# Attention with key chunks of 128: the last 64 keys of two head pairs on four quarters of the array, sums of four heads at once, order laid out by four heads

## The chip, the cores and the metric

The kernel runs on one core of one Trainium2 chip. The metric is the device time of one execution in microseconds. Each kernel was executed several times; all executions told of here are in the fast state (with one core there is nothing to tell a slow one by except its time, and all executions of each kernel lie within 0.5% of each other). The profile is one such execution. Its span runs from the first to the last instruction and is some 2 us shorter than the device time (1043.4 against 1045.3 us for the kernel before). Comparisons of stages below use spans, comparisons of kernels use device times.

## The reference, cut to what matters

Attention with normalised queries and keys, then a feed-forward block with the activation SoLU, all in fp32:

```python
# q, k, v: (8, 12, 448, 64)
q_n, k_n = rmsnorm(q, g_q), rmsnorm(k, g_k)
scores = scale * np.matmul(q_n, k_n.transpose(0, 1, 3, 2))      # 448 x 448 for each of 96 heads
attn = np.exp(scores - scores.max(-1)); attn /= attn.sum(-1)
x = np.matmul(attn, v)                                          # then (3584 tokens, 768)
h = x @ w_in                                                    # 768 -> 1024
u = layernorm(h * softmax(h)) * g_ln
out = u @ w_out                                                 # 1024 -> 768
```

## The kernel before

Heads go in pairs, 48 of them: 64 channels of one head lie on partitions 0 to 63, of the other on 64 to 127. A pair runs through a long pipeline: load q and k; squares (ScalarE); row sums (VectorE); their exchange and fold (GpSimd); an inverse square root (ScalarE, GpSimd); normalise (GpSimd); transpose (VectorE); the query's gain (ScalarE); scores (TensorE, a head on each row half); exponentials E (ScalarE); additions of the E of several chunks (VectorE, GpSimd); values and sums (TensorE, a head on each column half); division (VectorE). 448 keys are four chunks of 112. Token tiles of the feed-forward are woven in between. The first 12 pairs stand beside the conversion of w_in to the form that the kernel uses (early stage), the next 10 beside that of w_out and the first product of the feed-forward (middle), the rest has all of the feed-forward (late), and a tail has the last token tiles alone.

The order of instructions is laid out by hand, and each engine takes its own in that order.

```python
def load(n):                       # q and k of pair n: eight transfers, all on SyncE's queue
    d["qk"] = loads.tile([P, 2, NB, 32], FP32, tag="qk", name="qk", bufs=3)
    for s, src in enumerate((q, k)):
        for g in range(4):
            nc.sync.dma_start(d["qk"][g * 32 : g * 32 + 32, s], src[...])
def squares(n):                    # ScalarE, the first that reads q and k
    nc.scalar.activation(d["sq"], d["qk"]..., AF.Square)
def gain(n):                       # ScalarE, the last before the scores
    nc.scalar.activation(d["qkT"][:, 0], d["qkT"][:, 0], AF.Copy, scale=gcol[:, KF : KF + 1])
...
for n in range(N):                 # 48 pairs
    unit(lambda: scores(n, 0))
    ...
    unit(lambda: scores(n, 1))
    step(); step()                 # conversion of weights: VectorE's bits
    for _ in stages:
        load_next()                # the next weights, on SyncE's queue
    ...
    unit(lambda: values(n - 1))
    rsqrt_seed(n + 2)
    if n + 3 < N: squares(n + 3)   # of a pair whose load was given a pair earlier
    if n + 4 < N: load(n + 4)
    ...
    unit(lambda: sums(n - 1))
    later(1, lambda n=n: divide(n - 1))
    load_v(n + 1); begin(n + 1)
    gain(n + 1)
    unit(lambda: scores(n, 2)); unit(lambda: scores(n, 3))
```

`unit` gives TensorE a group of matmuls and counts it; `later(2, f)` gives f two units later. Note that `load(n + 4)` stands behind `squares(n + 3)`: a load has a whole pair's time before the squares that need it.

## Time and profile before

| | before |
|---|---|
| device time, median of 3 (lowest, highest) | 1045.52 us (1043.67, 1045.69) |
| span of the profiled execution, mean granted clock of TensorE | 1043.4 us, 0.992 |
| ramp, to the start of the third pair | 44.6 us |
| early stage, 10 pairs | 84.4 us |
| middle stage, 10 pairs | 135.75 us |
| late stage and tail | 778.7 us |

The prediction shows the lines of the page and the cut into stages. At its borders the first scores of the next pair, about 1.9 us, are already done; the table's borders lie that much earlier. One more row of the groups of instructions matters (line, engine, operation, shapes and count; busy us and mean ns; us of idle just before them with what ended it):

```profile
L537 ACT ACTIVATE sq<-qk 128x896 f32<-128x896 f32 x48 | 45.6, 950 | 6.1 <-DMA qk<-in_k_dram 2.5 <-issue 0.9 <-DVE tmp L469 0.4
```

Over the whole kernel ScalarE idles 6.1 us ahead of the squares, and 2.5 of them for a load.

### The profile page before, as it was taken

Reading aid. Unit: us, or ns where it says so; the run is one execution under the profiler, and the core shown is the slowest. Engines: PE = TensorE matmul, PEld = TensorE weight load, DVE = VectorE, ACT = ScalarE, POOL = GpSimd, SP = SyncE. Lnnn points to the kernel's source line nnn. Section 1 sums busy time; section 2 is a strip of 40 time slices with the busy share of each in tenths; the row PEclk is TensorE's granted clock in tenths of the full one; section 3 lists DMA queues with packets and bytes.
Section 4 is the critical chain, followed back from the end, with each engine's and each line's share of the span. In section 5 each row is a group of like instructions: output and inputs, shape, how many; then the busy total and the mean of one; then the engine's idle time right before and its main releaser. Section 6 shows DMA issues by size and latency. Waiting matters only on the chain.

```text
span 1043.4 us, 10599 instructions
## 1 busy us (share of the span) xinstructions
PE 991.1 (95%) x3571; PEld 445.0 (43%) x3571; DVE 541.4 (52%) x821; ACT 378.3 (36%) x645; POOL 293.9 (28%) x554
## 2 busy tenths in 40 slices
PE   2899999899999999999999999999999999999997
PEld 0233333333344444444444444444444444455554
DVE  3899977768633553344543344443344443556430
ACT  3788775455423223223223232322232222111110
POOL 4544564454622222222222222222233130000000
PEclk9999999899999999999999999999999999999999
DMA  7666663343411111111111111111110002134430
GB/s 151 132 141 143 138 125 89 76 89 68 72 42 41 42 27 42 41 42 42 41 27 42 42 41 42 42 26 42 42 42 24 9 25 84 43 133 116 133 106 34
DMA packets 234425, 70.09 MB, mean 67 GB/s; under 512 B 223600, under 2 KB 223608, under 8 KB 234360
## 3 DMA queue, kind: packets, MB, share of 16 engines
q1 hardware_dynamic: 230016, 58.23, 25.7%
q10 hardware_dynamic: 4344, 11.08, 2.7%
q8 instruction: 30, 0.49, 0.2%
q14 instruction: 35, 0.29, 0.1%
HBM read 58.27 MB, written 11.01 MB: 66 GB/s over the span
## 4 chain that ended last, share of the span: by engine, by line
PE 85%; ACT 5%; DVE 4%; POOL 2%; SPq 1%; issue 1%; DMA 1%; ACTq 0%; POOLq 0%; DVEq 0%
PE po L725 28%; PE h L670 26%; PE s L599 12%; PE o L627 12%; PE sm L638 4%; ACT E L602 3%; PE pu L714 2%; SPq L523 1%; DVE es L618 1%; POOL qkn L576 1%; POOL es L616 1%; ACT uT L715 1%; DMA raw<-in_moe_w_out_dram 1%; DVE bs L692 0%; POOL ss L551 0%
## 5 line engine op out<-in xcount | busy, mean ns | idle before, releaser
L670 PE MATMUL h<-w_in,xT 128*128 128x512 f32 x672 | 302.5, 600 | 0.0
L725 PE MATMUL po<-w_out,uT 128*128 128x384 f32 x896 | 299.4, 490 | 2.1 <-ACT uT L715 2.1
L725 PEld LDWEIGHTS po<-w_out,uT 128*128 128x128 f32 x896 | 167.5, 190 | 134.8 <-issue 17.1
L602 ACT ACTIVATE E<-s 112x896 f32<-112x896 f32 x192 | 165.8, 912 | 109.9 <-PE s L599 109.5
L599 PE MATMUL s<-qkT 64*112 64x448 f32 x768 | 177.2, 579 | 25.6 <-ACT qkT L590 12.3
L670 PEld LDWEIGHTS h<-w_in,xT 128*128 128x128 f32 x672 | 124.0, 190 | 163.9 <-issue 158.5
L627 PE MATMUL o<-E,v 112*64 112x448 f32 x768 | 155.1, 546 | 2.9 <-ACT uT L715 2.9
L698 POOL TENSOR_TENSOR he<-he,mhalf 128x1 f32<-128x1 f32 x28 | 22.8, 815 | 437.8 <-DVE he L697 437.8
L618 DVE TENSOR_TENSOR es<-es,E 112x896 f32<-112x896 f32 x72 | 78.4, 1088 | 82.0 <-ACT E L602 44.3
L599 PEld LDWEIGHTS s<-qkT 64*112 64x112 f32 x768 | 60.7, 176 | 131.3 <-issue 64.6
L726 ACT COPY y<-po 128x384 f32<-128x384 f32 x56 | 26.8, 479 | 234.1 <-PE po L725 234.1
L716 DVE COPY uT<-pu 128x512 f32<-128x512 f32 x28 | 19.3, 689 | 146.9 <-ACT uT L715 91.7
L683 ACT ACTIVATE u<-h,hmax 128x1024 f32<-128x1024 f32 x28 | 31.2, 1113 | 173.2 <-DVE hmax L680 173.2
L627 PEld LDWEIGHTS o<-E,v 112*64 112x64 f32 x768 | 50.9, 137 | 99.9 <-issue 85.2
L576 POOL TENSOR_TENSOR qkn<-qk,ny 128x896 f32<-128x896 f32 x48 | 81.4, 1696 | 24.2 <-DVE qkT L586 11.2
L542 DVE TENSOR_REDUCE part<-sq 128x28 f32<-128x896 f32 x48 | 51.2, 1066 | 65.4 <-ACT sq L537 65.4
L680 DVE TENSOR_REDUCE hmax<-h 128x1 f32<-128x1024 f32 x28 | 34.2, 1223 | 85.3 <-PE h L670 85.3
L616 POOL TENSOR_TENSOR es<-E 112x896 f32<-112x896 f32 x36 | 74.8, 2079 | 0.0
L568 POOL TENSOR_TENSOR nx<-nx,ny 128x28 f32<-128x28 f32 x48 | 14.2, 295 | 191.7 <-ACT ny L564 191.7
L638 PE MATMUL sm<-es,ones 112*64 112x448 f32 x240 | 54.3, 548 | 10.5 <-DVE es L618 9.9
L586 DVE STREAM_TRANSPOSE qkT<-qkn 128x896 f32<-128x896 f32 x48 | 53.0, 1103 | 5.2 <-POOL qkn L576 5.2
L688 DVE TENSOR_TENSOR u<-h,u 128x1024 f32<-128x1024 f32 x28 | 34.3, 1225 | 31.4 <-ACT u L683 31.3
(67 smaller groups left out, 650.5 us busy)
## 6 DMA issues: line engine op xcount, KB each, us to landing
raw<-in_moe_w_in_dram SPq DMA_DIRECT2D x24, 512.0 KB, 4.0
raw<-in_moe_w_out_dram SPq DMA_DIRECT2D x32, 384.0 KB, 3.2
qk<-in_q_dram SPq DMA_DIRECT2D x192, 56.0 KB, 2.7
qk<-in_k_dram SPq DMA_DIRECT2D x192, 56.0 KB, 2.2
v<-in_v_dram SPq DMA_DIRECT2D x48, 224.0 KB, 2.9
out_dram<-y ACTq DMA_DIRECT2D x28, 384.0 KB, 2.3
grow<-in_g_q_dram ACTq DMA_DIRECT2D x2, 0.2 KB
grow<-in_g_k_dram ACTq DMA_DIRECT2D x2, 0.2 KB
```

The costliest lines, as they stand in the source:

```text
L542: nc.vector.tensor_reduce(d["part"], d["sq"], AX, OP.add)
L576: nc.gpsimd.tensor_tensor(d["qkn"], d["qk"].rearrange("p s b d -> p (s b) d"), d["y"].rearrange("p b -> p b ()").to_broadcast([P, 2 * NB, ...
L586: nc.vector.transpose(d["qkT"].rearrange("p s t -> p (s t)"), d["qkn"].rearrange("p b d -> p (b d)"))
L599: nc.tensor.matmul(s[:, h, 0:S], d["qkT"][hh, 1, kc * SP : (kc + 1) * SP], d["qkT"][hh, 0, :], start=True, stop=True)
L602: nc.scalar.activation(d["E"][:, kc], s[:, :, 0:S], AF.Exp)
L616: nc.gpsimd.tensor_tensor(d["es", 3], d["E"][:, 0], d["E"][:, 1], OP.add)
L618: nc.vector.tensor_tensor(d["es", 3], d["es", 3], d["E"][:, kc], OP.add)
L627: nc.tensor.matmul(d["o"][h * D : (h + 1) * D, :], d["v"][:, h, kc], d["E"][:, kc, h], start=(kc == 0), stop=(kc == NJ - 1),)
L638: nc.tensor.matmul(d["sm"][h * D : (h + 1) * D, :], ones[0:SP, :], es[:, h], start=(i == 0), stop=(i == len(tiles) - 1),)
L670: nc.tensor.matmul(d["h"][:, hs], xTs[m][:, c, i * P : (i + 1) * P], w_in[:, c, hs], start=(c == 0), stop=(c == KD - 1))
L688: nc.vector.tensor_tensor(u, d["h"], u, OP.mult)
L725: nc.tensor.matmul(po, d["uT"][:, c], w_out[:, c, hs], start=(c == 0), stop=(c == KF - 1))
```

## The change

The intent is fewer steps on TensorE. Each pair keeps three full chunks of 128 keys. The last 64 keys of two pairs a and b form one shared chunk, computed on four 64 x 64 quarters of the array. Row sums of four heads are taken at once on four column quarters. As two pairs now share work, the order is laid out by quads (two pairs, four heads), 24 of them. The diff, cut to its core:

```diff
-    NJ = 4
-    SP = S // NJ
+    NJ = S // P                                   # 3 chunks of 128
+    NQ = B * NP // 2
...
-        d["qk"] = loads.tile(..., tag="qk", name="qk", bufs=3)
+        d["qk"] = loads.tile(..., tag="qk", name="qk", bufs=4)
...
+    def scores_last(m):
+        s = ps_t.tile([P, 2, 512], FP32, tag="t", name="s")
+        for i in range(2):
+            for h in range(2):
+                nc.tensor.matmul(s[i * D : (i + 1) * D, h, 0:S], qkT[hh, 1, NJ * P : S], qkT[hh, 0, :], ...)
+        exponentials(quads[m], NJ, s)
+    def values_last(m):
+        for h in range(2):
+            for i in range(2):
+                nc.tensor.matmul(st[2 * m + i]["o"][h * D : (h + 1) * D, :], d["vl"][pp, h], d["E", NJ][pp, h], ...)
+    def sums(m):
+        for x, term in enumerate(terms):           # one term late, three early
+            for h in range(2):
+                for i in range(2):
+                    g = 32 * (2 * h + i)
+                    nc.tensor.matmul(sm[g : g + 32, :], w, e[:, h], ...)
+    def inverse(m): ...                            # one transpose, one reciprocal, four copies on GpSimd
+    def divide(m): ...                             # for both pairs
...
-        for n in range(N):
+        for m in range(NQ):
+            a, b = 2 * m, 2 * m + 1
+            unit(lambda: scores(a, 0)); ...        # a: 0, 1, 2, then scores_last(m); b: 0, 1, 2
+            step(b)
+            unit(outputs)                          # values_last(m), values(a)
+            load(a + 4)
+            squares(a + 4)
+            row_sums(a + 4)
+            end(b)                                 # the next weights' load waits for b's bits on VectorE
+            qk_transpose(a + 2)
+            ...
+            unit(lambda: values(b))
+            load(b + 4)
+            squares(b + 4)
+            row_sums(b + 4)
+            gain(a + 2)
+            ...
+            unit(lambda: sums(m))
+            later(1, lambda m=m: inverse(m))
+            later(2, lambda m=m: divide(m))
```

Besides, the first keys come on ScalarE's DMA queue, VectorE does the first pair's normalisation, and the check of the weights at the end reads tiles of 448.

## The prediction

> **What bounds the kernel now.** I read the page from the top: the busy line, then the slices, to see whether one limit holds throughout.
>
> ```profile
> PE 991.1 (95%) x3571; PEld 445.0 (43%) x3571; DVE 541.4 (52%) x821; ACT 378.3 (36%) x645; POOL 293.9 (28%) x554
> ...
> PE   2899999899999999999999999999999999999997
> ...
> DVE  3899977768633553344543344443344443556430
> ACT  3788775455423223223223232322232222111110
> ```
>
> TensorE is busy for 95% of the span, and short of it only in the first slices. VectorE and ScalarE are nearly full in the first eighth and half idle later. So there are stages with different limits. I cut the span where the groups of matmuls change (windows view; PE, PEld, DVE, ACT, POOL busy, clock, DMA):
>
> ```profile
> 16.00:46.50 30.50, 22.72 (x88) 7.50 (x88) 21.72 (x25) 22.25 (x39) 18.14 (x40) 0.89 0.63 133
> 46.54:130.87 84.33, 81.68 (x403) 28.17 (x401) 78.52 (x110) 67.24 (x111) 41.39 (x101) 1.00 0.66 140
> 130.87:266.62 135.75, 125.30 (x470) 46.27 (x469) 102.14 (x161) 80.27 (x141) 68.67 (x114) 0.97 0.42 89
> 266.62:901.59 634.97, 628.05 (x2195) 289.10 (x2194) 277.39 (x403) 188.12 (x318) 158.89 (x277) 1.00 0.17 40
> ```
>
> These are the ramp, the early stage (attention alone beside the conversion of w_in), the middle (one half of the first product per pair), and the late stage (all). In the late stage TensorE idles 1%: only fewer matmul steps help there. In the early stage VectorE is at 93% and ScalarE at 80%: they follow closely.
>
> The timeline of TensorE gives the price of each piece. The early stage repeats this:
>
> ```profile
> 65.43 1.82 PE L599 MATMUL s<-qkT 64*112 64x448 f32 x8 [0.27 <-ACT E L602]
> 67.17 3.23 PE L627 MATMUL o<-E,v 112*64 112x448 f32 x16
> 70.23 1.67 PE L638 MATMUL sm<-es,ones 112*64 112x448 f32 x8
> 71.83 1.76 PE L599 MATMUL s<-qkT 64*112 64x448 f32 x8
> 73.86 1.82 PE L599 MATMUL s<-qkT 64*112 64x448 f32 x8 [0.27 <-ACT E L602]
> ```
>
> Every fp32 matmul leaves two records (384 score matmuls in the program, x768 on the page), so I count passes. The difference of starts counts, since a record's end holds a tail of about 0.2 us. Values: 16 passes in 70.23 - 67.17 = 3.06 us, which is 8 steps of 0.376 us and 0.05 for the change of form. So two passes, one per head, always run at once. Sums: 8 passes, 1.60 us, four steps and 0.10. Scores: 8 passes, 67.17 - 65.43 = 1.74 us, and when undisturbed 1.69, so 0.845 us for a chunk of two heads (a slot). A run of four slots takes 75.61 - 71.83 = 3.77 us with the next values' start at 75.61, because the third waits for the exponentials of the first: two score buffers. One pair costs 8.43 us.
>
> In the middle there are waits:
>
> ```profile
> 159.91 3.23 PE L627 MATMUL o<-E,v 112*64 112x448 f32 x16
> 165.13 0.97 PE L638 MATMUL sm<-es,ones 112*64 112x448 f32 x4 [1.99 <-DVE es L618]
> ...
> 194.43 1.76 PE L638 MATMUL sm<-es,ones 112*64 112x448 f32 x4 [3.42 <-DVE es L618]
> ```
>
> The sums wait for an addition that stands on VectorE behind the moments of a token tile. Ten pairs take 135.75 us; their own steps are 10 x (3.38 + 3.06 + 0.85) + 9 x 5.35 for the halves of the first product = 121 us, so some 14 us are waits.
>
> **What the Trainium skill says.** "TensorE: Matmul & The Clock Gate", Measured speedup vs the span model: matmuls on different tiles of the array run together, the span of a pack being one matmul plus about 4 ns per further tile; 16 tiles gave 10.6 times. "TensorEngine Tiling (Array Packing)", Available Configurations and Key Properties: 64x64 gives four tiles and 128x32 four, tiles work independently, and a change of tiling mode drains the engine. The same page, Gotcha 1: row tiles must write different PSUM banks. The trace agrees for two tiles (8 steps for 16 passes) and shows the change of mode at 0.05 to 0.10 us. No row of it shows four tiles at once: that is the bet. The changed code does put its quarters as the gotcha asks: the two row halves go to different banks.
>
> **The change, part by part.** It takes 448 keys as three chunks of 128, and the last 64 of two pairs as one chunk on four quarters. Per two pairs (a quad):
>
> Scores: 8 slots become 6 + 1 = 7. Values: 8 slots become 7. Sums: in the late and middle stages four passes for each pair on two column halves become eight on four column quarters, so 4 steps become 2; in the early stage 8 steps become 6, as chunk 2 and the shared chunk go straight to TensorE and the second addition per pair leaves VectorE. Exponentials: 8 of 0.91 us become 7. Division: one transpose of the sums for four heads in place of two (0.64 us), one reciprocal less, but four copies on GpSimd of about 0.22 us. Weights of 128 columns in place of 112 load beside the matmuls, as now.
>
> Late stage. Per quad TensorE saves a score slot (0.8), two value steps (0.75) and two sum steps with a change of form (0.85): 2.4 us. The built order has four groups of feed-forward work per quad where there were six: two groups fewer, each with about 0.2 us of form changes (h takes 5.35 us between attention groups, 5.15 among its own kind), 0.4. Two new forms cost 0.1: net 2.7. Twelve and a half quads: 33.7 us. All on the path, with VectorE at 44%.
>
> Middle. A quad: a run of four slots 3.87, a run of three 2.9, values 14 x 0.376 + 0.15 = 5.4, sums 0.85, and 1.8 x 5.35 = 9.6: 22.6 us. It gains nothing in scores (3.87 + 2.9 against 4 x 1.69), as longer runs wait on exponentials. The additions now stand before, not behind, the token tile's moments, so I expect the 2 to 3.4 us waits to go; but the exponential of a token tile (1.11 us behind a maximum of 1.22) falls into the run of four: I allow 2 us. 24.6 against 135.75 / 5 = 27.15: 2.55 us, five times, 12.7.
>
> Early. A run of seven slots at 2.03 us per two (73.86 - 71.83) and one last of 0.87: 7.0, with a gain of 0.66 us between the exponentials some 7.4; values 5.4; sums 6 x 0.376 + 0.1 = 2.4: 15.2 against 16.86, 1.66 us, five times, 8.3.
>
> Ramp. Now the first score stands at 16.27 us and the second pair's sums end at 46.54, with about 1.9 us of scores of the third pair done by then: 44.6. Afterwards the first keys come on a second queue (the first squares near 5.5 us, not 7.17), VectorE does the first normalisation in place of GpSimd (1.1, not 1.69 us), but the second row sum and the gains stand before the first transpose: first score near 14.4. Second chain: gain near 20, then ScalarE is the limit with seven exponentials, two conversions of 1.4 and two squares: last exponential near 29.5, sums finished near 36. Gain 8.5 us.
>
> Tail: the same instructions, 0. Sum: 33.7 + 12.7 + 8.3 + 8.5 = 63.2. For drains that I can't see and rows that don't mesh I take 3 off: 60. 1045.5 - 60 = 985 us.
>
> **Rivals.** (1) Four quarters run only two at a time, for instance because the two passes of a matmul follow each other in order. Then every pack costs two more steps: late and middle three packs per quad, 18 x 2.26; early five packs, 6 x 3.76; 63 us come back: 1045, no change. Against it: two tiles already mesh perfectly, and the skill's sixteen. For it: no row of this trace. (2) VectorE and ScalarE become the limit early and in the middle. By my count VectorE has 12.8 of 15.2 us per early quad; in its fixed order a late row sum delays the next transpose, and TensorE waits at each quad's border. If both stages gain nothing but the removed waits: about 1000. (3) New waits late: both output banks are held from the shared chunk until a division that goes VectorE, GpSimd, VectorE (about 5 us after the sums), and the output chunk needs both banks at once. The work between (6 to 10 us of feed-forward) should hide it; at 1 us per quad it would be 24 us: 1009. (4) The ramp gains nothing, the wait moving from GpSimd to ScalarE: 993.
>
> **Range and chances.** 970 to 1012 holds the sum with rivals 2 to 4 in part; below 970 would need all waits gone. Rival 1 I give 8%. Two per cent is 1024.6 us: faster 0.91, within 0.07, slower 0.02.
>
> **What would show it.** First step: the shared scores' eight passes start to start in about 0.85 us, and late sums of eight passes in 0.85 us; 1.6 means rival 1. Late: the stretch to the last attention sums shorter by about 34 us, TensorE at 98% or more there. Middle: no 2 us wait of sums for VectorE. Early: about 15.2 us per quad; 16.9 with waits for the query's gain means rival 2. Ramp: first score at 14.4, first quad's sums finished at 36. Waits of the output matmuls for the division mean rival 3. The prediction is wrong if a pack takes over 1.2 us, or waits late sum to over 20 us.

## The result, and the profile after

| | before | after |
|---|---|---|
| device time, median of 4 (lowest, highest) | 1044.6 us (1043.6, 1045.69) | 1053.07 us (1052.25, 1053.97) |
| span, mean granted clock | 1043.4 us, 0.992 | 1052.2 us, 0.966 |

The ratio is 1.0081, with a 95% interval of 1.0064 to 1.0099: a little slower, and within 2%. A ratio here is the mean time of one kernel's runs over that of the other's of the same rounds, so not quite the ratio of the medians.

The page of the changed kernel, its busy line and two rows of 40 slices:

```profile
PE 965.3 (92%) x3619; PEld 428.6 (41%) x3619; DVE 536.9 (51%) x771; ACT 362.4 (34%) x621; POOL 318.4 (30%) x642
...
PE   3797887788699999999999999999999999999997
...
PEclk9799998898699999999999999999999999999999
```

TensorE's work fell by 26 us (991.1 to 965.3), as intended, and yet the span is 8.8 us longer: its idle time rose from 52 to 87 us. The second row says where: before, it was at 8 or more tenths in all slices but the first and the last; now five of the second to eleventh are at 6 or 7. From the twelfth on all but the last are at 9 again. The same in the windows view (window, its us; busy us of PE, PEld, DVE, ACT, POOL with counts; granted clock, DMA share, GB/s), cut where quads begin: ramp, early, middle, late without the tail.

```profile
15.00:43.48 28.48, 19.16 (x89) 5.69 (x89) 11.35 (x14) 16.60 (x30) 14.28 (x30) 0.86 0.62 135
43.48:139.16 95.68, 80.98 (x440) 26.37 (x440) 69.33 (x91) 63.97 (x105) 48.31 (x120) 0.92 0.58 124
139.16:298.70 159.54, 129.37 (x469) 44.22 (x469) 113.94 (x157) 79.69 (x139) 75.75 (x134) 0.86 0.38 79
298.70:904.81 606.11, 596.96 (x2182) 275.31 (x2181) 275.83 (x376) 180.41 (x309) 175.00 (x334) 1.00 0.17 39
```

In the early stage no engine is full: TensorE 85%, VectorE 72%, ScalarE 67%. They wait for each other, or for something that is none of them. Against the prediction, stage by stage (us of span, equal work in each row):

| | before | predicted | after | after - before | after - predicted |
|---|---|---|---|---|---|
| ramp | 44.6 | 36 | 43.5 | -1.1 | +7.5 |
| early | 84.4 | 76 | 95.7 | +11.3 | +19.7 |
| middle | 135.75 | 123 | 159.5 | +23.8 | +36.5 |
| late and tail | 778.7 | 745 | 753.5 | -25.2 | +8.5 |
| sum | 1043.4 | 980 | 1052.2 | +8.8 | +72.2 |

The predicted column is the prediction's own terms, without its allowance of 3 us. The late gain came, for the most part; the first third lost 34 us where 29.5 were to be gained.

**What an early quad waits for.** TensorE's timeline (start, us, engine, line, operation, tiles, shapes; in brackets the idle time before, and who ended it):

```profile
82.41 4.17 PE L636 MATMUL s<-qkT 64*128 64x448 f32 x12 [2.69 <-ACT qkT L622]
86.50 1.11 PE L648 MATMUL s<-qkT 64*64 64x448 f32 x8
...
90.58 0.98 PE L675 MATMUL o<-E,vl 64*64 64x448 f32 x8
...
97.68 0.93 PE L711 MATMUL sm<-es,ones 128*32 128x448 f32 x8
101.85 1.40 PE L636 MATMUL s<-qkT 64*128 64x448 f32 x6 [3.24 <-ACT qkT L622]
```

First, the bet of the prediction: the eight records of the shared values take 91.49 - 90.58 = 0.91 us from start to the next group's start, against 1.50 for four steps on two tiles. Late in the trace the four records of a pack start at 427.868, 427.875, 427.881 and 427.888 us. The four quarters run at once. Second, each early quad begins with an idle 2.3 to 3.2 us (4.8 us the first one), until the query's gain (L622) is there. The gain's own story is on ScalarE, and its input's on VectorE:

```profile
100.29 0.95 ACT L564 ACTIVATE sq<-qk 128x896 f32<-128x896 f32 x1 [5.40 <-DMA v<-in_v_dram]
101.15 0.65 ACT L622 ACTIVATE qkT<-qkT,gcol 128x448 f32<-128x448 f32 x1
```

```profile
96.20 1.10 DVE L618 STREAM_TRANSPOSE qkT<-qkn 128x896 f32<-128x896 f32 x1
```

The transpose that the gain reads was done at 97.30. The gain ran at 101.15, directly behind the squares of pair b + 4 of the quad after next, which nobody needs for a long time. ScalarE had been idle for 5.40 us ahead of these squares. The Trainium skill ("TensorE: Matmul & The Clock Gate", Architectural detail) calls ScalarE's and VectorE's queues strict FIFO, and the trace agrees: the gain's data stood ready for 3.85 us, most of it with the engine idle. The profile infers a load of v, given right behind k, as the releaser; but the squares read only q and k. What held those is on SyncE's queue of transfers:

```profile
92.87 0.35 SPq L458 DMA_DIRECT2D raw<-in_moe_w_in_dram  x1
93.32 1.94 SPq L543 DMA_DIRECT2D qk<-in_q_dram  x4
95.31 2.92 SPq L543 DMA_DIRECT2D qk<-in_k_dram  x4
```

The load of the next weights waits until VectorE has read the old ones (its step ended at 92.80), and q and k of pair b + 4 stand behind it in the queue. They take 0.49 to 0.73 us each to issue, eight of them 4.9 us, and some 2.2 us (the page's median for k) to land: 98.23 + 2.2 = 100.4, which is when the squares ran. In the kernel before the same queue had the same order, and the same late weights:

```profile
68.94 0.35 SPq L449 DMA_DIRECT2D raw<-in_moe_w_in_dram  x1
69.38 1.95 SPq L523 DMA_DIRECT2D qk<-in_q_dram  x4
```

but the squares at that moment read what had been loaded a pair earlier, and the gain followed without delay:

```profile
68.76 0.95 ACT L537 ACTIVATE sq<-qk 128x896 f32<-128x896 f32 x1
...
70.96 0.65 ACT L590 ACTIVATE qkT<-qkT,gcol 128x448 f32<-128x448 f32 x1
```

Over the whole kernel the row of the squares, which had 6.1 us of idle before it, now has:

```profile
L564 ACT ACTIVATE sq<-qk 128x896 f32<-128x896 f32 x48 | 45.5, 949 | 67.7 <-DMA v<-in_v_dram 31.4 <-DVE part L569 21.5 <-DMA qk<-in_k_dram 13.9
```

45.3 us of it are for transfers. In the middle the same wait is 1.4 to 4.9 us, the longest here:

```profile
202.67 1.86 PE L636 MATMUL s<-qkT 64*128 64x448 f32 x4 [4.87 <-ACT qkT L622]
```

So the theory, called A in the expectations: the change gave up the lead of a load over its squares (`load(b + 4); squares(b + 4)` stand next to each other, where before a pair lay between), and the fixed order of ScalarE passes the wait on to the gain, and so to TensorE. The Trainium skill ("DMA: Bandwidth & Descriptors", Rules for kernel authors) has the rule: "Issue the DMA early, do compute, wait on its semaphore late". Rivals: B, the engines are simply full and any order gives this; the transfers themselves are too slow; the lowered clock (0.86 in the middle) is a cause and not a consequence.

### The profile page after: what moved, and what is told of

Read it like the earlier page. It is cut to its first block, busy times and chain, and to the rows that moved or that the text cites. A ratio compares the mean times of both kernels' runs of the same rounds, so it can differ in the third digit from the quotient of the medians.

```text
span 1052.2 us, 10821 instructions
## 1 busy us (share of the span) xinstructions
PE 965.3 (92%) x3619; PEld 428.6 (41%) x3619; DVE 536.9 (51%) x771; ACT 362.4 (34%) x621; POOL 318.4 (30%) x642
## 4 chain that ended last, share of the span: by engine, by line
PE 74%; DVE 6%; ACT 5%; SPq 5%; POOL 4%; DMA 3%; issue 2%; ACTq 0%; POOLq 0%; DVEq 0%
PE po L809 27%; PE h L754 25%; PE s L636 10%; PE o L686 6%; SPq L543 4%; PE s L648 2%; PE pu L798 2%; ACT E L629 2%; DMA v<-in_v_dram 2%; POOL qkn L608 1%; PE sm L711 1%; PE o L675 1%; ACT sq L564 1%; POOL es L662 1%; DVE qkT L618 1%
## 5 line engine op out<-in xcount | busy, mean ns | idle before, releaser
L636 PE MATMUL s<-qkT 64*128 64x448 f32 x576 | 155.2, 646 | 60.3 <-ACT qkT L622 36.4
L629 ACT ACTIVATE E<-s 128x896 f32<-128x896 f32 x168 | 149.6, 915 | 93.8 <-PE s L636 87.7
L665 DVE TENSOR_TENSOR es<-es,E 128x896 f32<-128x896 f32 (+1 forms) x72 | 78.4, 1089 | 96.0 <-ACT E L629 65.3
L662 POOL TENSOR_TENSOR es<-E 128x896 f32<-128x896 f32 x36 | 76.3, 2118 | 158.4 <-ACT E L629 158.3
L686 PE MATMUL o<-E,v 128*64 128x448 f32 x576 | 114.0, 545 | 0.0
L636 PEld LDWEIGHTS s<-qkT 64*128 64x128 f32 x576 | 52.0, 205 | 150.8 <-ACT E L629 49.8
L800 DVE COPY uT<-pu 128x512 f32<-128x512 f32 x28 | 19.3, 688 | 160.1 <-PE pu L798 92.2
L686 PEld LDWEIGHTS o<-E,v 128*64 128x64 f32 x576 | 39.3, 138 | 74.4 <-issue 72.7
L564 ACT ACTIVATE sq<-qk 128x896 f32<-128x896 f32 x48 | 45.5, 949 | 67.7 <-DMA v<-in_v_dram 31.4
L582 POOL COPY ss<-part 32x28 f32<-32x28 f32 x188 | 40.1, 213 | 45.7 <-DVE part L569 26.7
L600 POOL TENSOR_TENSOR nx<-nx,ny 128x28 f32<-128x28 f32 x47 | 24.5, 521 | 89.1 <-ACT ny L595 89.1
```

The lines of the kernel that those rows point to most:

```text
L564: nc.scalar.activation(d["sq"], d["qk"].rearrange("p s b d -> p (s b) d"), AF.Square)
L629: nc.scalar.activation(d["E", kc], s[:, :, 0:S], AF.Exp)
L636: nc.tensor.matmul(s[:, h, 0:S], d["qkT"][hh, 1, kc * P : (kc + 1) * P], d["qkT"][hh, 0, :], start=True, stop=True)
L662: e.tensor_tensor(d["es"], d["E", 0], d["E", 1], OP.add)
L665: nc.vector.tensor_tensor(d["es"][pp], d["es"][pp], x[pp], OP.add)
L686: nc.tensor.matmul(d["o"][h * D : (h + 1) * D, :], d["v"][:, h, kc], d["E", kc][:, h], start=False, stop=(kc == NJ - 1),)
```

## The experiments

All kernels below give the reference's result. The kernel before ran on the same chip each time, with medians of 1045.15 to 1045.43 us. Clear of the 2% are only 8 and 9 (faster) and 10 (slower); the intervals of 1 and 5 reach across 0.98, so by the 2% rule these two are unclear, and 2, 3, 4, 6 and 7 are within it. Differences to the changed kernel's 1053.07 us are between rounds; the medians of the kernel before moved by under 1 us between these.

**1. Loads first.** Both loads go to the start of the quad, more than half a quad ahead of their squares; nothing else changes.

```diff
+            if m + 2 < NQ:
+                load(a + 4)
+                load(b + 4)
             unit(lambda: scores(a, 0))
...
             unit(outputs)
             if m + 2 < NQ:
-                load(a + 4)
                 squares(a + 4)
...
             unit(lambda: values(b))
             if m + 2 < NQ:
-                load(b + 4)
                 squares(b + 4)
```

> The changed kernel with the query and key loads of the quad after next issued at the start of the quad, ahead of the weight loads, and nothing else moved. Theory A (the loads stand in the queue behind weight loads that wait for VectorE; the squares right behind them hold ScalarE, and the next quad's gain stands behind the squares): the waits of the scores for the gain go; early quads 19.1 -> 15.5 to 16.5 us, the middle 12 us shorter, the ramp 3 us; 1053 -> 1015 to 1030. Theory B (VectorE and ScalarE are simply full in these stages): within 8 us of 1053. Theory C (the halved clock after the waits is most of it): cannot be told from A here, see the run that fills the wait.

Measured: 1024.34 us (1024.06 to 1024.99), ratio to before 0.98 (0.9784 to 0.9816). The squares' wait for transfers went from 45.3 to about 5 us (the 25.0 us for row sums don't hold TensorE at an early border, as the lines after show):

```profile
L564 ACT ACTIVATE sq<-qk 128x896 f32<-128x896 f32 x48 | 45.5, 948 | 31.1 <-DVE part L569 25.0 <-DMA qk<-in_q_dram 3.5 <-DMA raw<-in_moe_w_out_dram 1.4
```

and the border of two quads has no wait (TensorE's timeline, then the windows of early and middle):

```profile
116.69 0.93 PE L711 MATMUL sm<-es,ones 128*32 128x448 f32 x8
117.56 0.65 PE L636 MATMUL s<-qkT 64*128 64x448 f32 x2
```

```profile
38.09:117.56 79.47, 77.70 (x445) 24.73 (x441) 68.31 (x90) 62.31 (x104) 53.75 (x120) 1.00 0.70 148
117.56:267.62 150.06, 124.54 (x472) 43.29 (x469) 113.40 (x156) 78.98 (x139) 78.09 (x139) 0.90 0.40 84
```

The ramp became 5.4 us shorter, the early stage 16.2, the middle 9.5, and the late stage and tail 2.1 longer: 29.0 together. Theory A holds, and two loads moved turn the change from a small loss to a gain of 2%. Early, TensorE is busy 98% at full clock. The middle is only partly mended.

**2. The gain first.** The load stays late, and only the gain goes ahead of the squares.

```diff
             unit(lambda: values(b))
+            if more:
+                gain(a + 2)
             if m + 2 < NQ:
                 load(b + 4)
                 squares(b + 4)
                 row_sums(b + 4)
-            if more:
-                gain(a + 2)
```

> The changed kernel with the gain of the next quad's first pair placed ahead of the squares that wait for the load, loads left where they are. Theory A: the first scores of a quad start 2 to 3 us sooner, but the first exponential still stands behind the squares, so only part comes back: 1053 -> 1038 to 1047. Theory B: unchanged, 1050 to 1056.

Measured: 1049.91 us (1048.74 to 1051.19), ratio 1.0042. That is 3 us below the changed kernel, less than theory A's figure and within 0.1 us of theory B's, so this run alone would not tell them apart. The row of the scores, first of the changed kernel, then of this one, says why:

```profile
L636 PE MATMUL s<-qkT 64*128 64x448 f32 x576 | 155.2, 646 | 60.3 <-ACT qkT L622 36.4 <-ACT E L629 18.7 <-DVE r L719 3.5
```

```profile
L636 PE MATMUL s<-qkT 64*128 64x448 f32 x576 | 150.4, 626 | 62.2 <-ACT E L629 36.5 <-DVE r L719 15.2 <-ACT qkT L622 8.8
```

The wait for the gain fell by 27.6 us, and the waits for the exponentials and for the division rose by 29.5. Whatever is placed behind late squares waits with them: first the gain, now the exponentials. The expectation had named the first exponential as standing behind the squares too, but put far too little of the wait on it.

**3. Both loads before the weights.** The load of b goes directly behind that of a, so ahead of the weights' load, but still only one group of matmuls ahead of its own use.

```diff
                 load(a + 4)
+                load(b + 4)
                 squares(a + 4)
...
             if m + 2 < NQ:
-                load(b + 4)
                 squares(b + 4)
```

> The changed kernel with the load of the second pair directly behind that of the first, so ahead of the one weight load that waits for VectorE; the first load is not moved. Theory A: the second load lands some 3 us sooner in each early and middle quad; 1053 -> 1025 to 1038, less than with both loads at the start. If the transfers themselves were too slow (a rival: DMA bandwidth), it and the run with the loads first would gain under 5 us.

Measured: 1031.07 us (1030.75 to 1031.81), ratio 0.9864 (0.9848 to 0.9881). This gets 22 of the 29 us. So most of the loss is the place behind the weights' load in the queue; the transfers themselves are quick enough. The other 7 us I put down to lead; no run separates them.

**4. The wait filled.** Three matmuls of no use stand ahead of the first scores of a quad in the middle, to keep TensorE's clock up.

```diff
     def scores(n, kc):
+        if kc == 0 and n % 2 == 0 and W_IN < n < W_OUT:
+            for x in range(3):
+                nc.tensor.matmul(s[:, 0], w_in[:, 0, 0:P], w_in[:, 1, 0:512], start=True, stop=True)
```

> The changed kernel with three useless matmuls of 128x512 (about 2.6 us, overwritten by the scores) in the wait before the first scores of the quads of the middle stage (pairs 14 to 21). Theory A: the wait is for data, the fill ends inside it in two of four quads; the clock may stay up, worth at most 2 us a quad as ScalarE and VectorE set the pace there: 1045 to 1056. Theory C (the halved clock is most of the middle's loss): the four runs of scores at 7.4 us fall to 4 us: 1033 to 1043.

Measured: 1054.22 us (1053.4 to 1055.0), ratio 1.0084. The windows view has the middle at 160.1 us and a clock of 0.91, against 159.5 us and 0.86 in the changed kernel. The clock rose and the time didn't fall. In the second quad of the middle the run of scores that began the quad takes 9.09 us at a clock of 0.73, against 9.10 us at 0.57 in the changed kernel: what the matmuls saved, the waits for exponentials took. So the low clock is not what sets the time of these runs. The fill raised it only in part, though: three of the next products still take 6.2 to 6.4 us in place of 5.4, and what that costs this run doesn't show.

**5. The token tile's exponential later** (on top of 1). In the middle the exponential of a token tile (1.11 us, behind a maximum on VectorE) goes to ScalarE one unit later, behind the next scores' exponentials.

```diff
         later(1, lambda: ff_max(t))
+        later(2 if middle else 1, lambda: ff_exp(t))
```

> Loads first, and in the middle stage the exponential of a token tile is given to ScalarE one unit later, behind the first exponential of the next quad. Theory D (with the loads first, the middle is still long because the first exponentials of a quad stand behind that of the token tile, which waits for a maximum on VectorE): 1024 -> 1014 to 1020. Rival E (VectorE is full in the middle, whatever the order): within 3 us of the kernel with the loads first.

Measured: 1022.88 us (1022.35 to 1023.7), ratio 0.9787: 1.5 us less than 1, what rival E of the expectation says (experiment 9 will speak against E). In the second quad of the middle the run of scores of the first pair fell from 7.39 to 5.59 us, and that of the second rose from 3.05 to 5.30. The prediction's 2 us "for the token tile" are not the middle's problem.

**6. Sums by pair** (on top of 1). From pair 12 on the sums of four heads are undone: 64 columns of ones, two column halves, twice.

```diff
+        if not early:
+            for i in range(2):
+                for h in range(2):
+                    nc.tensor.matmul(sm[h * D : (h + 1) * D, i, 0:S], ones64, st[2 * m + i]["es"][:, h], ...)
+            return
```

> Loads first, and from pair 12 on the sums of four heads at once undone: four matmuls on column halves, two at a time, into two banks, and one transpose of the sums more on VectorE in place of the four copies on GpSimd. If the column quarters are worth their two steps (0.75 us) in each of the 13 late quads and little in the middle: 1024 -> 1032 to 1042. If they were hidden: within 4 us.

Measured: 1038.01 us (1037.26 to 1038.75), ratio 0.9929. The sums of four heads are worth 13.7 us over 18 quads. That this makes 0.76 us each, just two steps of 0.376, is partly chance. By the windows 8.7 us fall to the late stage and tail (0.67 us per quad) and 5.0 to the middle (0.99), where the second scores of a quad wait 1.5 to 2.1 us for the transpose of the sums, against 1.0 to 1.1 in 1: the edit also gives VectorE a transpose and a reciprocal more.

**7. Last keys by pair** (on top of 1). The shared chunk is undone: each pair takes its last 64 keys by itself, in scores and values. This also costs one more exponential per quad.

```diff
-            unit(lambda: scores_last(m))
+            unit(lambda: scores_last(m, 0))
...
             unit(lambda: scores(b, 2))
+            unit(lambda: scores_last(m, 1))
```

> Loads first, and the last 64 keys of each pair scored, exponentiated and multiplied by themselves, away from those of the other pair, so two quarters of the array at a time: one score slot (0.85), two steps of values (0.75) and one exponential (0.91) more per quad. If the shared chunk is worth that on the path: 1024 -> 1050 to 1068. If TensorE had slack: under 1035.

Measured: 1051.59 us (1050.51 to 1053.55), ratio 1.0065. The shared chunk is worth 27 us, in all stages: by the windows 14.2 in the late stage and tail, 6.8 in the middle and 5.3 early. Experiments 6 and 7 together: both packs on four tiles pay, though the changed kernel as a whole gained nothing.

**8. Exchange of sums behind the inverse** (on top of 5). Early, the shared values waited 0.8 us for the division of the last quad, whose four copies stood on GpSimd behind the exchange of row sums of pair b + 4.

```diff
-            if m + 2 < NQ:
-                swap_sums(b + 4)
-                fold_sums(b + 4)
             unit(lambda: sums(m))
             later(1, lambda m=m: inverse(m))
+            if m + 2 < NQ:
+                later(1, lambda b=b: (swap_sums(b + 4), fold_sums(b + 4)))
```

> As the run with the token exponential later, and GpSimd's swaps of the pair after next placed behind the copies of the inverse sums, so that the division no longer stands behind them. The early quads' wait of the shared values for the division (0.77 us in four of five) goes: 2 to 5 us under the run with the token exponential later. If that wait is caused elsewhere: within 1.5 us of it.

Measured: 1020.98 us (1020.31 to 1021.83), ratio 0.9767; 1.9 us below 5, just short of what was expected. The early stage takes 77.1 us. Its middle shows what is left there. ScalarE's timeline:

```profile
154.03 0.61 ACT L487 ACTIVATE w_out<-tmp,gcol 128x384 f32<-128x384 f32 x1 [5.02 <-DVE tmp L482]
154.55 0.63 ACT L473 ACTIVATE tmp<-raw,seven 128x384 f32<-128x384 uint32 x1
...
156.73 1.71 ACT L629 ACTIVATE E<-s 128x896 f32<-128x896 f32 x2
```

ScalarE idles 5 us for the conversion of a weight tile on VectorE (L482), then does 2.7 us of conversion, and only then the exponentials of scores that had started at 153.56. TensorE has two score buffers and waits 2.35 us. It is the same pattern as the gain behind the squares: something nobody needs soon stands ahead of something that TensorE needs now.

**9. Conversion behind the exponentials** (on top of 8). In the middle the conversion's last step and the next tile's first go behind the first two exponentials of pair b, and with them the load of the next weights.

```diff
-            else:
+            elif a < W_IN:
                 end(a)
-                if a >= W_IN:
-                    begin(b)
+            else:
+                step(a)
...
             unit(lambda: scores(b, 1))
             if a >= W_IN:
+                for _ in sets[a]:
+                    load_next()
+                step(a)
+                begin(b)
```

> As the run with the swaps behind the inverse, and in the middle stage the product of the weight conversion (which waits on ScalarE for VectorE's join) and the low bits of the next conversion are given to ScalarE behind the first two exponentials of the second pair, not ahead of them. Theory F (what is left of the middle's length is ScalarE's fixed order, conversions ahead of exponentials): 1021 -> 1008 to 1016. Rival E (VectorE's total sets the middle): 1018 to 1023.

Measured: 1013.62 us (1010.72 to 1014.86), ratio 0.97 (0.9675 to 0.9726). This is the best version, and beats both kernels. Its middle takes 140.2 us, from 149.7 in 8:

```profile
115.30:255.48 140.18, 119.91 (x469) 42.44 (x469) 118.02 (x156) 78.73 (x139) 76.14 (x139) 0.96 0.43 90
```

VectorE is now at 84% there, and TensorE at 86% at a clock of 0.96. Rival E, VectorE's total, gave 1018 to 1023 and fell.

**10. The kernel before with a short lead.** The cross-check from the other side: nothing of the change, only the load put directly ahead of its squares.

```diff
-        load(3)
         begin(0)
...
             if n + 3 < N:
+                load(n + 3)
                 squares(n + 3)
-            if n + 4 < N:
-                load(n + 4)
```

> The kernel before, with the one thing of the changed order that theory A blames: each pair's queries and keys are loaded directly ahead of their squares, not one pair earlier. Theory A: the old kernel then shows the same waits of scores for the gain, some 2 to 4 us in each pair of the early and middle stages: 1045 -> 1065 to 1110. If the lead of the loads does not matter: within 5 us of 1045.

Measured: 1153.86 us (1152.94 to 1155.74), ratio 1.1047 (1.1027 to 1.1067): the direction of A, and more than expected (1065 to 1110). All of the loss is ahead of the late stage: the group that begins the late stage starts at 375.83 us, against 266.62 in the kernel before, and from there to the end it takes 776.5 us against 776.8. Its list of waits (engine and line, what it waited for, us in total, times, longest):

```profile
ACT sq L537 <- DMA qk<-in_k_dram: 149.7, 22, 12.6
```

The 2.5 us of before have become 149.7. The sign was not the expected one: the scores wait for the gain no longer than before (12.5 us in total, 12.3 before), but for exponentials 87.7 us (11.0 before). In this order these stand behind the late squares, so it is the same handing on as in experiment 2. The lead alone, without any packing on the array, makes or breaks the first part of this kernel.

## Why the prediction was wrong

The predicted time was 985 us (970 to 1012), and the result 1053. The spans of the versions by stage, against the prediction's terms:

| | predicted | after | 1: loads first | 9: best |
|---|---|---|---|---|
| ramp | 36 | 43.5 | 38.1 | 38.2 |
| early | 76 | 95.7 | 79.5 | 77.1 |
| middle | 123 | 159.5 | 150.1 | 140.2 |
| late and tail | 745 | 753.5 | 755.6 | 755.4 |
| sum | 980 | 1052.2 | 1023.2 | 1010.9 |

- **Bound by TensorE's steps, late: right.** The late rows show no wait in most quads, and undoing either pack costs time there (experiments 6 and 7).
- **Four quarters at once: right.** 0.91 us per pack against the predicted 0.85, and rival 1 (1.6) fell with the first look at the trace.
- **Late, 33.7 us: right mechanism, size off.** Measured 25.2. Two of the late quads, five apart, show the same row of waits: the sums wait for an addition that stands behind a token tile's moments on VectorE, and the second output product waits for the inverse:

```profile
433.44 0.94 PE L711 MATMUL sm<-es,ones 128*32 128x448 f32 x2
435.14 0.95 PE L711 MATMUL sm<-es,ones 128*32 128x448 f32 x6 [0.76 <-DVE es L665]
436.02 5.43 PE L809 MATMUL po<-w_out,uT 128*128 128x384 f32 x16
443.17 5.43 PE L809 MATMUL po<-w_out,uT 128*128 128x384 f32 x16 [1.72 <-DVE r L719]
```

  The sums take 436.02 - 433.44 = 2.58 us in place of 0.89, and the product waits 1.72: 3.4 us, and again at 677.00. The second wait is of rival 3's kind, but for the bank of the sums and not for the output banks. These 6.8 us don't explain the 8.5 that are missing, since the kernel before had waits of its own here. By the windows, from the first late quad to the end, TensorE's idle time rose by 2.2 us (15.7 to 17.9), and its busy time fell by 27.4 (763.0 to 735.6) where the steps were to give 33.7. Some 1.9 of these 6.3 are the two held-up sums, so about half of the 8.5 is waits, net of the old ones, and half is the steps, mis-sized. Against experiment 1, undoing the sums adds 0.63 us of busy time per late quad where I had 0.85; undoing the shared chunk adds 1.59 where I had 1.55, and in time less only because waits go (idle 11.8 us against 18.2). The chunk was sized right, the sums too high, and by this estimate little is left of the 0.4 for two groups of feed-forward work fewer. Also, the late stage has 13 quads, not twelve and a half: at 2.7 us the sum was 35.1.
- **Early, 8.3 us to be gained: wrong, 11.3 lost.** The step that failed is "A run of seven slots ... 15.2 against 16.86". The matmul count in it was right: with the loads first the first quad of the stage takes 15.26 us, and the stage comes to 77.1 us in version 9. What failed is the unspoken premise that everything a quad reads is there when it begins. I counted the busy time of VectorE and ScalarE and the steps of TensorE, and never followed the eight transfers of a pair from their place in the order to the squares. The diff shows it: `squares(n + 3)` ahead of `load(n + 4)` before, `load(b + 4)` directly ahead of `squares(b + 4)` after, and a weights' load that waits for VectorE ahead of it in the queue. The four qk buffers in place of three, which look like more lead, hid this from me: more buffers give no lead when the load is given late.
- **Middle, 12.7 us to be gained: wrong, 23.8 lost.** 9.5 us of the 36.5 between prediction and result are the late loads (experiment 1), 9.9 more came with experiments 5, 8 and 9, nearly all with the conversion that stood ahead of exponentials. The step "I allow 2 us" for what falls into the run of four scores was mis-sized: not the token tile's exponential but the conversion's place, and it is larger. 17 us stay open in version 9. From the second quad of the middle on its timeline has waits of the first scores for the gain (0.4 to 1.5 us), of the next for the transpose of the sums (1.1), of the shared scores for exponentials behind a token tile's maximum (1.7 in three quads), one of 5.0 us for an exponential behind a conversion in the last quad, and some time at a lowered clock; I did not test these apart. One rival I overlooked: in the middle VectorE is busy for 113.9 us in the changed kernel, against 102.1 before, with four instructions fewer. Six of its conversion steps (L477, L478) last 1.9 to 2.2 us there, the others of these lines 0.3 to 0.6, and each of the six runs beside a long operation of GpSimd, as here (VectorE, then GpSimd):

```profile
276.00 2.23 DVE L477 TENSOR_SCALAR tmp<-raw 128x384 uint32<-128x384 uint32 x1
```

```profile
275.90 2.11 POOL L662 TENSOR_TENSOR es<-E 128x896 f32<-128x896 f32 x1
```

  In the middle of the kernel before no conversion step of VectorE takes over 0.7 us. ScalarE waits for these conversions (5.02 us in experiment 8), so part of the middle's loss, and of the 17 us, may be the new order putting the two engines' work side by side. No run tests it.
- **Ramp, 8.5 us: wrong, 1.1 gained.** The first score came at 15.43 us (predicted 14.4), but the second quad began at 43.5. With the loads first it begins at 38.1. So 5.4 us of the missing 7.5 are the same cause.
- **Tail, 0: right.** From the start of the last sums to the end it is 141.8 us before and 147.4 after, but the changed kernel has one more half of an output product there (5.3 us).
- **Rival 2 named the symptom and missed the cause.** It said that "TensorE waits at each quad's border", and the last part of the prediction gave "waits for the query's gain" as its sign. The sign came, 36.4 us of it. But its reason was VectorE and ScalarE at their limit, and the windows show them at 72% and 67%, with ScalarE idle for 5.4 us ahead of the squares. I had also capped it at "about 1000" us, since I thought the worst was no gain in those stages. A fixed order that waits for a transfer can lose more than the whole gain.

The chance of 0.02 for a loss over 2% was not tested, as the result is within 2%; but 0.07 for "within" was too small for an order rewritten in full that I had checked only by counts of work.

## What to carry to other kernels

When a change rewrites the order of a kernel, follow each load from its place in the order to the first instruction that reads it, and ask what stands ahead of it in its queue and what stands behind its reader on the reader's engine; a count of steps and busy time shows none of this. A wait for data that nobody needs soon becomes a wait of the bounding engine when something urgent is placed behind it, and moving that one thing ahead only hands the wait to the next in line (experiment 2): move the load instead. And a change that comes out even can be a good change with a bad order in it: two moved loads made it 2% faster than the kernel before, a few more moves 3%.

## What the Trainium skill lacked or had wrong

- "DMA: Bandwidth & Descriptors" (Anatomy of one DMA) gives a sequencer's dispatch as about 50 ns, for the path through GpSimd. For copies issued from SyncE on trn2 the page has no time (a table about trn3 has 512 sequencer cycles per copy for "previous generations"). Here a transfer of 32 partitions of q or k took 0.49 to 0.73 us of SyncE's queue (four in 1.94 and 2.92 us), so eight of them hold up the queue for 4.9 us. The issue itself is worth counting.
- The same page says (Anatomy of one DMA) that a semaphore wait happens on the issuing sequencer, but its rule to issue early (Rules for kernel authors) doesn't draw the conclusion that a wait ahead in the same queue undoes it. Here a weights' load that waited for VectorE held eight transfers that waited for nothing, and moving them ahead of it was worth 22 us (experiment 3).
- "TensorE: Matmul & The Clock Gate" (Why this matters for your kernels) asks for no idle gaps over about 3 us; elsewhere (A second HAM failure mode) the page tells of a clock that falls with short gaps, without giving their length. In experiment 1 the clock was 0.50 for 6.8 us around a longest gap of 2.46 us, behind a stretch of 3.4 us in which TensorE was busy for 1.39:

```profile
143.90:147.30 3.40, 1.39 (x6) 0.30 (x4) 3.35 (x5) 0.52 (x1) 2.04 (x10) 0.99 0.68 110
147.30:154.10 6.80, 5.26 (x14) 1.64 (x15) 6.47 (x13) 4.69 (x7) 1.44 (x2) 0.50 0.42 68
```

- The same page (Measured speedup vs the span model) has about 4 ns for each further tile of a pack; the trace shows 6 to 7 ns between the starts of the four records, which changes nothing here.
- "TensorEngine Tiling (Array Packing)" (Key Properties) says that a change of tiling mode drains the engine and gives no price. Here eight passes in another form take 0.91 us from start to next start, where two steps of 0.376 would be 0.75: some 0.15 us for going into the form and out of it.
- "FP8 and Floating Point Precision" counts four passes for true fp32 and gives no time. Here an fp32 matmul of 448 columns leaves two records 0.376 us apart, and two or four matmuls on different tiles share these two steps.
